# By-token rows: v loaded once a batch into a ring of pairs, turned tiles in six named places, and splits and pieces tied to the score tiles

## The chip, the cores and the metric

One core of one Trainium2 chip. The metric is device time in microseconds (us) of one execution, the median of several runs.

## The reference

For each of 8 batches of 2496 tokens, with u and v of 256 columns and z of 64:

```
scores = (1/S) * z @ z.T
out    = u * (max(scores, 0)**2 @ v)          # x, 19968 rows of 256
logits = normed(x) @ normed(expert_emb).T / tau     # 8 experts
y[t]   = p_top(t) * (max(x[t] @ w1[e], 0) @ w2[e])  # e = the token's best expert
```

The expert part is computed for the best expert of each token alone, so tokens have to be sorted by expert.

## The kernel before

**Two stages.** The first stage computes attention batch by batch, gates it with u and routes each token: its row goes by an indirect DMA into a table sorted by expert. The second stage runs the experts over slots of that table. The change is in the first stage.

**Numbers in pairs.** Each float32 operand is split into two float16 parts (high and low), after a scaling by a power of two. So z has tiles z1 and z2 (`z_split`), v has rows `vv` of high and low parts (`v_split`, ScalarE writes the high part, VectorE the low), and the squared scores have `hl` (`parts`). The scaling needs the largest absolute value of z and of v of the whole batch before the first split: `scan_load` brings a piece of z or v, `scan_max` reduces it, and `scale_pieces` makes the power of two, with two small matmuls in between.

**Steps.** A batch is 5 groups g of (up to) 512 tokens, and each group runs over 20 rows s of 128 keys: 100 steps a batch, 800 in all. The `for i, (b, g, q, s)` loop is the program order; PE follows it exactly. A step multiplies one tile of squared scores with a row of v (`values`, L361 to L370). Since scores are symmetric, only tiles with s // 4 >= g are computed (`scores`: L269 and L270 on PE, L272 and L273 on ScalarE; `parts`: L306 and L307 on VectorE, L302 and L303 for the short group). Those are 20, 16, 12, 8 and 4 of the 20 steps of the five groups; they are made three and two such steps ahead. For the tiles of later groups SP sends a transposing DMA (L319, L321) from `hl` into `tt`, which a later group reads. So the first group of a batch computes 20 tiles and turns 18 of them, the last computes four and turns none.

**Beside the steps.** For the next batch, a list `todo` made by `ahead` holds pieces with a step at which they are due: scans, scale pieces, z loads, z splits and z copies. v comes twice: 8 scan loads of 320 KB a batch (L107, reduced on L114), then 20 row loads of 128 KB (`v_load`, L201) into 6 buffers `vt`, each load four rows ahead of its split (L238, L239). `queue` holds the pieces of the routing of the last group (L411 to L525), among them four transposing DMAs of the gated rows (L449, `rowt`). `wq` holds the preparation of the expert weights (L562 to L625).

**Who sets the order.** PE is in program order. On the other engines and on SP, which issues nearly all DMAs, a scheduler orders the instructions by when it believes them ready; `tc.issue_after(x)` makes instructions stand behind x on their engine. Before, `todo` pieces stand behind the latest score tile on ScalarE and VectorE (`state["at"]`, `state["dv"]`), and `u` and weight DMAs behind the latest transposing DMA (`behind_moves`). Row loads, splits of v and `queue` pieces are free. Each engine and each DMA queue then takes its instructions strictly in that order.

Of the kernel before, what the change touches and what calls it, by code (L numbers as in the profile page):

```python
# [7 lines left out]
F32 = mybir.dt.float32  # L8
# [11 lines left out]
P = 128  # L20
# [3 lines left out]
VAHEAD = 4  # L24
# [20 lines left out]
def relu2_attention_then_moe(ctx, tc, zT, u, v, emb, tau, w1, w2, ident, tri, iota_e, out):  # L45
# [46 lines left out]
    zraw = {}  # L92


    ZSCANS, VSCANS = 2, 2 * D // DQ
    SCAN = SP * DQ // (P * ZSCANS)
    assert SP * DQ == ZSCANS * SCAN * P and DQ % ZSCANS == 0 and SP % VSCANS == 0
    scan = {}

    def scan_load(b, what, i, eng=None):  # L100

        t = wk.tile([P, SCAN], F32, name="scan", tag="scan", bufs=2)
        if what == "z":
            src = zT[b, i * (DQ // ZSCANS):(i + 1) * (DQ // ZSCANS), :]
        else:
            src = v[b, i * (SP // VSCANS):(i + 1) * (SP // VSCANS), :]
        (eng or nc.sync).dma_start(t, src.rearrange("a c -> (a c)").rearrange("(p w) -> p w", p=P))  # L107
        scan[b, what, i] = t

    def scan_max(b, what, i):  # L110
        if i == 0:
            n = ZSCANS if what == "z" else VSCANS if b else NV0
            scan[b, what] = sml.tile([P, n], F32, name="smx" + what)
# [3 lines left out]
    SCANS = [("z", i) for i in range(ZSCANS)] + [("v", i) for i in range(VSCANS)]  # L117
# [44 lines left out]

    def z_tiles(b):
# [12 lines left out]
    def z_split(b, c0):  # L176
# [7 lines left out]
        nc.scalar.activation(z1[lo, c], zt[lo, :w], AF.Copy, scale=k[lo])  # L184
        if b == 0:
            nc.scalar.activation(z2[hi, c], zt[hi, :w], AF.Copy, scale=k[hi])
        nc.vector.scalar_tensor_tensor(z2[lo, c], zt[lo, :w], k[lo], z1[lo, c], op0=ALU.mult, op1=ALU.subtract)
# [9 lines left out]
    vraw = {}  # L197
# [6 lines left out]
    VC = 4  # L204
    NV0 = ceil_div(NST, VC)
    v0 = []

    def v_first(i):

        if not v0:  # L210
            assert NST * D <= 3 * min(W1, W2)
            v0.extend([wp.tile([P, W1], F32, name="v0a", tag="wr1"), wp.tile([P, W2], F32, name="v0b", tag="wr2"),
                       wp.tile([P, 2 * max(W1, W2)], F16, name="v0c", tag="wo").bitcast(F32)])
        per = min(W1, W2) // D
        assert per % VC == 0
        q = i * VC
        n = min(VC, NST - q)
        t = v0[q // per][:, q % per * D:(q % per + n) * D].rearrange("p (j d) -> p j d", d=D)
        nc.sync.dma_start(t, v[0, q * P:(q + n) * P, :].rearrange("(j p) d -> p j d", p=P))
        for j in range(n):  # L220
            vraw[0, q + j] = t[:, j, :]
        scan[0, "v", i] = t.rearrange("p j d -> p (j d)")

    def v_split(b, s):
        vt = vraw.pop((b, s))
        vv = vring.tile([P, 2 * D], F16, name="vv", tag="vv")
# [10 lines left out]
        else:  # L237
            nc.scalar.activation(vv[:, 0:D], vt, AF.Copy, scale=k)  # L238
            nc.vector.scalar_tensor_tensor(vv[:, D:], vt, k, vv[:, 0:D], op0=ALU.mult, op1=ALU.subtract)  # L239
        Vs[b, s] = vv  # L240

    state = {"pm": False, "sp": None}

    def behind_moves():
        return tc.issue_after(state["sp"]) if state["sp"] else ExitStack()
# [3 lines left out]
    turned = {}  # L249
    joint = {}  # L250
# [13 lines left out]
    def scores(b, g, s):  # L264
# [7 lines left out]
        state["at"] = nc.scalar.activation(a[:, :n], sc[:, :n], AF.Relu, scale=2.0 ** -SHIFT).ins  # L272
# [12 lines left out]
    def parts(b, g, s, a):  # L285
# [12 lines left out]
        else:  # L298
# [3 lines left out]
            state["dv"] = nc.vector.tensor_copy(hl[:, :n], a[:, :n]).ins  # L302
# [3 lines left out]
        state["dv"] = nc.vector.tensor_copy(oh, src).ins  # L306
# [926 lines left out]
```

## Time and profile before

| | us |
|---|---|
| median of 3 runs | 2185.7 |
| lowest and highest run | 2184.86, 2188.75 |
| the profiled execution, its own time | 2187.64 |
| its span in the profile | 2185.9 |
| first stage, to the first expert matmul | 1340.4 |
| second stage | 845.5 |

The span leaves out 1.7 us of the execution's own time. PE's busy share is 96%, but matmuls are pipelined and their ends are modelled, so how full PE is has to be read from how long equal amounts of matmuls take. The stretches below are cut at the first `acc` matmul of a batch or of a group.

### The profile page before, as it was taken

The page shows a single profiled execution, that of the slowest core. Times are in us where ns is not written, and L with a number is a line of the kernel's source. Part 1 is how long each engine was busy: PE and PEld are TensorE (multiplying, and loading weights), DVE is VectorE, ACT ScalarE, POOL GpSimd, SP SyncE. Part 2 cuts the span into 40 slices and gives each one's busy share as a digit, 9 for nine tenths or more (in the row PEclk, how much of TensorE's full clock was granted, in tenths as well). Part 3 has the DMA queues.
Part 4 walks back from the last instruction along what each step waited for, and adds up shares of the span by engine and source line. Part 5 has one row for each costly group of instructions (what it writes and reads, how often), then busy time and mean ns, then how long its engine had stood idle before and what let it go on. Part 6 is the DMA issues. An engine that isn't in the chain of part 4 may idle for free.

```text
span 2185.9 us, 50968 instructions
## 1 busy us (share of the span) xinstructions
PE 2103.3 (96%) x19210; PEld 1779.6 (81%) x19210; DVE 1334.7 (61%) x3976; ACT 1017.4 (47%) x2131; POOL 332.0 (15%) x344
## 2 busy tenths in 40 slices
PE   6999999999999999999999999999999999999998
PEld 4787787787777777787777788888888888888898
DVE  8777887887877877876877865533333333333333
ACT  7566566566566566666656653222222222222221
POOL 0011011101101111011011011212111121111111
PEclk9999999999999999999999999999999999999999
DMA  7977988989978978988977877433333333247584
GB/s 179 204 167 184 213 175 191 215 170 189 215 152 186 198 173 176 196 186 173 191 168 159 161 151 180 128 86 89 81 65 88 88 91 57 50 110 201 130 215 116
DMA packets 668860, 335.99 MB, mean 154 GB/s; under 512 B 564662, under 2 KB 637375, under 8 KB 662465
## 3 DMA queue, kind: packets, MB, share of 16 engines
q1 hardware_dynamic: 653136, 291.06, 61.8%
q0 software_dynamic: 15184, 41.24, 6.8%
q8 instruction: 152, 2.49, 0.5%
q14 instruction: 100, 0.81, 0.1%
q10 hardware_dynamic: 288, 0.39, 0.1%
HBM read 273.46 MB, written 59.60 MB: 152 GB/s over the span
## 4 chain that ended last, share of the span: by engine, by line
PE 69%; DVE 13%; DMA 10%; issue 3%; ACT 3%; SPq 2%; another core or an unknown queue 0%; DVEq 0%; POOL 0%; POOLq 0%; ACTq 0%
PE acc L361 8%; PE acc L365 8%; PE acc L363 8%; PE po L974 6%; PE po L972 6%; PE po L973 6%; DMA scan<-in_v_dram 4%; PE sc L270 2%; PE sc L269 2%; DVE smxv L114 1%; DMA zt<-in_zT_dram 1%; SPq L449 1%; DVE vv L239 1%; DVE x L411 1%; DMA vt<-in_v_dram 1%
## 5 line engine op out<-in xcount | busy, mean ns | idle before, releaser
L272 ACT ACTIVATE a<-sc 128x512 f32<-128x512 f32 (+1 forms) x480 | 267.7, 558 | 242.9 <-PE sc L270 155.7
L525 POOL DMA_INDIRECT xs<-row,dsti x160 | 171.0, 1069 | 1075.6 <-ACT row L445 318.2
L273 ACT ACTIVATE a<-a 128x512 f32<-128x512 f32 (+1 forms) x480 | 286.3, 596 | 12.6
L361 PE MATMUL acc<-vv,tt 128*128 128x256 f16 x1152 | 269.2, 273 | 0.5 <-DVE lg L462 0.4
L363 PE MATMUL acc<-vv,tt 128*128 128x256 f16 x1152 | 269.1, 272 | 0.5 <-issue 0.5
L979 POOL DMA_INDIRECT out_dram<-ot,me x159 | 155.1, 975 | 659.2 <-DVE ot L978 626.0
L972 PE MATMUL po<-w,hh 128*128 128x256 f16 x928 | 253.0, 273 | 0.0
L974 PE MATMUL po<-w,hl 128*128 128x256 f16 x928 | 253.0, 273 | 0.0
L973 PE MATMUL po<-w,hh 128*128 128x256 f16 x928 | 253.0, 273 | 0.0
L978 DVE TENSOR_SCALAR ot<-po,me,w 128x256 f32<-128x256 f32 x116 | 58.3, 540 | 215.5 <-PE po L974 205.5
L269 PE MATMUL sc<-z 128*128 128x512 f16 (+1 forms) x480 | 175.6, 366 | 9.5 <-ACT a L272 6.3
L365 PE MATMUL acc<-vv,tt 128*128 128x256 f16 x1152 | 178.2, 273 | 0.4 <-issue 0.4
L270 PE MATMUL sc<-z,z 128*128 128x512 f16 (+1 forms) x480 | 175.7, 366 | 0.0
L974 PEld LDWEIGHTS <-hl 128*128 128x128 f16 x1272 | 124.5, 98 | 14.5
L973 PEld LDWEIGHTS <-hh 128*128 128x128 f16 x1272 | 124.5, 98 | 14.2
L972 PEld LDWEIGHTS <-hh 128*128 128x128 f16 x1272 | 124.5, 98 | 14.2
L361 PEld LDWEIGHTS <-tt 128*128 128x128 f16 x1152 | 112.5, 98 | 14.3 <-DVE lg L462 0.9
L363 PEld LDWEIGHTS <-tt 128*128 128x128 f16 x1152 | 112.6, 98 | 13.9 <-issue 1.1
L365 PEld LDWEIGHTS <-tt 128*128 128x128 f16 x1152 | 112.6, 98 | 13.5 <-issue 0.5
L239 DVE SCALAR_TENSOR_TENSOR vv<-vt,scv,vv 128x256 f16<-128x256 f32 x133 | 61.4, 477 | 53.1 <-ACT vv L238 52.8
L974 PE MATMUL po<-wb,hl 128*128 128x256 f16 x344 | 93.8, 273 | 0.0
L972 PE MATMUL po<-wb,hh 128*128 128x256 f16 x344 | 93.8, 273 | 0.0
(5249 smaller groups left out, 5498.4 us busy)
## 6 DMA issues: line engine op xcount, KB each, us to landing
w<-wsd SPq DMA_DIRECT2D x64, 1026.0 KB
wa<-wsd SPq DMA_DIRECT2D x46, 1024.0 KB
w<-wsd SPq DMA_DIRECT2D x42, 1024.0 KB
wb<-wsd SPq DMA_DIRECT2D x24, 1026.0 KB
ut<-in_u_dram SPq DMA_DIRECT2D x72, 256.0 KB
vt<-in_v_dram SPq DMA_DIRECT2D x140, 128.0 KB
scan<-in_v_dram SPq DMA_DIRECT2D x56, 320.0 KB
wr<-in_w_dram SPq DMA_DIRECT2D x64, 256.0 KB
```

Of the source, the lines that this page charges most:

```text
L269: nc.tensor.matmul(sc[:, :n], z1[:, ss], z1[:, t0:t0 + n], start=True, stop=False)
L270: nc.tensor.matmul(sc[:, :n], z1[:, ss], z2[:, t0:t0 + n], start=False, stop=True)
L272: state["at"] = nc.scalar.activation(a[:, :n], sc[:, :n], AF.Relu, scale=2.0 ** -SHIFT).ins
L273: nc.scalar.activation(a[:, :n], a[:, :n], AF.Square)
L361: nc.tensor.matmul(outs[j], piece(ph, j), vh, start=first and j % 2 == 0, stop=False, skip_group_check=True)
L363: nc.tensor.matmul(outs[j], piece(ph, j), vl, start=False, stop=False, skip_group_check=True)
L365: nc.tensor.matmul(outs[j], piece(pl, j), vl if last else vh, start=False, stop=ends, skip_group_check=True)
L525: put = nc.gpsimd.indirect_dma_start(xs[:, :], bass.IndirectOffsetOnAxis(ap=loc["dsti"][:m, j:j + 1], axis=0), row[:m, j, :], None)
L972: nc.tensor.matmul(o, hh[:, f, t], wh, start=(f == 0), stop=False)
L973: nc.tensor.matmul(o, hh[:, f, t], wl, start=False, stop=False)
L974: nc.tensor.matmul(o, hl[:, f, t], wh, start=False, stop=(f == NF - 1))
L979: put = nc.gpsimd.indirect_dma_start(out, bass.IndirectOffsetOnAxis(ap=me.bitcast(U32)[:, j, 1:2], axis=0), ot[:, j, :], None, bounds_chec ...
```

## The change

`v` is loaded once a batch: `scan_load` for v brings two rows of 128 keys (256 KB) into a tile of the same ring `vring` that holds the split rows, `scan_max` reduces that tile, and `v_split` later reads it from there. The ring has 22 places for a raw or a split pair. Row loads and their 6 buffers are gone; the scan buffer is one of half the size, and z is scanned in four pieces instead of two.

```
-    vring = actx.enter_context(tc.tile_pool(name="vring", bufs=NST + 5))
+    NVP = NST // 2
+    vring = actx.enter_context(tc.tile_pool(name="vring", bufs=2 * NVP + 2))
-    tp = actx.enter_context(tc.tile_pool(name="tp", bufs=min(7, max(1, NG * (NG - 1) // 2))))
+    tp = actx.enter_context(tc.tile_pool(name="tp", bufs=1))
+    places = [f"tt{i}" for i in range(6)]
...
-    ZSCANS, VSCANS = 2, 2 * D // DQ
+    ZSCANS = 4
...
     def scan_load(b, what, i, eng=None):
-        t = wk.tile([P, SCAN], F32, name="scan", tag="scan", bufs=2)
...
+        if what == "v":
+            t = vring.tile([P, 2, D], F32, name="vr", tag="vv")
+            (eng or nc.sync).dma_start(t, v[b, 2 * i * P:2 * (i + 1) * P, :].rearrange("(j p) d -> p j d", p=P))
+            for j in range(2):
+                vraw[b, 2 * i + j] = t[:, j, :]
+            scan[b, what, i] = t.rearrange("p j d -> p (j d)")
+            return
+        t = wk.tile([P, SCAN], F32, name="scan", tag="scan", bufs=1)
...
-    def v_load(b, s):
-        vt = wk.tile([P, D], F32, name="vt", tag="vt", bufs=VAHEAD + 2)
-        nc.sync.dma_start(vt, v[b, s * P:(s + 1) * P, :])
-        vraw[b, s] = vt
```

A score tile's ScalarE work now stands behind the last split on ScalarE, and its VectorE work behind the last split on VectorE (`state["as"]` and `state["ds"]` are set in `z_split` and `v_split`, from the second batch's splits on). `todo` DMAs stand behind the latest transposing DMA, and `queue` and weight pieces behind the latest score tile:

```
+            if b:
+                state["as"], state["ds"] = hi_, lo_
...
+        with behind("as"):
+            state["at"] = nc.scalar.activation(a[:, :n], sc[:, :n], AF.Relu, scale=2.0 ** -SHIFT).ins
...
+        with behind("ds"):
+            state["dv"] = nc.vector.tensor_copy(oh, src).ins
...
-                with tc.issue_after(state["at"]), tc.issue_after(state["dv"]):
+                with tc.issue_after(state["at"]), tc.issue_after(state["dv"]), behind_moves():
                     todo.pop(0)[2]()
         values(accs[b, g], b, g, q, s, *half(b, g, s))
         if queue:
-            queue.pop(0)()
+            with tc.issue_after(state["at"]), tc.issue_after(state["dv"]):
+                queue.pop(0)()
...
-                with tc.issue_after(state["dv"]), behind_moves():
+                with tc.issue_after(state["at"]), tc.issue_after(state["dv"]), behind_moves():
                     wq.pop(0)()
```

The scans are due earlier and are spread wider, the splits of the next batch's v are due two steps ahead instead of four, and a turned tile takes the place that has been free longest of six, instead of a rotation of seven:

```
-    early = 4
+    early = 2
...
-        at = min(NST + 4, NB // 4)
-        for i, what in enumerate(SCANS):
-            todo.append((at + 2 * i, False, lambda w=what: scan_load(b + 1, *w)))
-            todo.append((at + 2 * i + 4, False, lambda w=what: scan_max(b + 1, *w)))
-        at += 2 * len(SCANS) + 4
+        for i in range(ZSCANS):
+            todo.append((6 * i, False, lambda i=i: scan_load(b + 1, "z", i)))
+            todo.append((6 * i + 5, False, lambda i=i: scan_max(b + 1, "z", i)))
+        for i in range(NVP):
+            todo.append((3 * i + 2, False, lambda i=i: scan_load(b + 1, "v", i)))
+            todo.append((3 * i + 14, False, lambda i=i: scan_max(b + 1, "v", i)))
+        at = 3 * NVP + 14
...
+                place_[b, g, h] = places.pop(0)
+                turned[b, g, h] = tp.tile([P, 2 * GT, 512], F16, name="tt", tag=place_[b, g, h])
...
+        if c == GT - 1:
+            places.append(place_.pop((b, h, g)))
```

At the start, the first batch's v comes in ten loads of 256 KB, five from SP and five from ScalarE's queue, instead of five of 512 KB from SP, and is reduced in ten pieces.

How the order moves is shown at three places.

ScalarE, at the end of the fifth batch (number 4), from the last rows of the last group to the first score tile behind them. `vv` and `vh` are the splits of the next batch's v, `row_100` a routing piece, `a<-sc` the score tile of the last own step. Before:

```order
L238 ACTIVATE vv<-vt,scv 128x256
L445 ACTIVATE row_100<-x,up 128x256
L238 ACTIVATE vv<-vt,scv 128x256 x5
L234 ACTIVATE vh<-vt,scv 64x256
L238 ACTIVATE vv<-vt,scv 128x256 x3
L232 ACTIVATE vv<-vt,scv 64x256
L272 ACTIVATE a<-sc 128x448
```

Now:

```order
L418 ACTIVATE sq,n_12937<-x 128x256 x3
L192 ACTIVATE z_10782<-zt,scz 64x256
L441 ACTIVATE row_100<-x,up 128x256 x3
L192 ACTIVATE z_10782<-zt,scz 64x256
L441 ACTIVATE row_100<-x,up 128x256
L263 ACTIVATE a<-sc 128x448
```

The splits of v no longer stand ahead of that tile. They are now in the fourth group of the batch, ahead of its first own score tile, again on ScalarE:

```order
L223 ACTIVATE vv<-vr,scv 128x256 x3
L441 ACTIVATE row_99<-x,up 128x256 x4
L219 ACTIVATE vh<-vr,scv 64x256
L618 ACTIVATE wo<-wr_10676,wup 128x512
L223 ACTIVATE vv<-vr,scv 128x256 x9
L217 ACTIVATE vv<-vr,scv 64x256
L263 ACTIVATE a<-sc 128x512
```

Before, four weight pieces stood at that place and five splits of v further ahead.

SP, in the first group of the next batch (number 5). `tt` are turned score tiles, `rowt` turned gated rows. Before:

```order
L319 DMA_TRANSPOSE tt<-hl__13692 128x8x128
L562 DMA wr_13360<-in_w_dram 128x512
L449 DMA_TRANSPOSE rowt<-row_99 128x4x128
L319 DMA_TRANSPOSE tt<-hl__13725 128x8x128
L449 DMA_TRANSPOSE rowt<-row_99 128x4x128 x3
L319 DMA_TRANSPOSE tt<-hl__13754 128x8x128
L319 DMA_TRANSPOSE tt<-hl__13802 128x8x128
L379 DMA ut<-in_u_dram 128x2x256
```

Now:

```order
L313 DMA_TRANSPOSE tt<-hl__13689 128x8x128
L445 DMA_TRANSPOSE rowt<-row_99 128x4x128
L313 DMA_TRANSPOSE tt<-hl__13715 128x8x128
L445 DMA_TRANSPOSE rowt<-row_99 128x4x128
L313 DMA_TRANSPOSE tt<-hl__13740 128x8x128
L445 DMA_TRANSPOSE rowt<-row_99 128x4x128
L107 DMA vr<-in_v_dram 128x2x256
L313 DMA_TRANSPOSE tt<-hl__13768 128x8x128
L445 DMA_TRANSPOSE rowt<-row_99 128x4x128
L114 DMA scan<-in_zT_dram 128x320
```

The turned rows come about five tiles later and one by one, and between the first and the last of the group's 16 `tt` transposes there are now six loads of v and two of z, with one more z load ahead of them, where none were.

## Rows read from the trace of the kernel before

**Rows 1.** The head of the profile's page: busy us of PE, its share of the span, and the row loads of v.

```profile
PE 2103.3 (96%) x19210; PEld 1779.6 (81%) x19210; DVE 1334.7 (61%) x3976; ACT 1017.4 (47%) x2131; POOL 332.0 (15%) x344
...
vt<-in_v_dram SPq DMA_DIRECT2D x140, 128.0 KB
```

**Rows 2.** The view of windows, one window for each batch (0 to 7): window, its length, then busy us and instructions of each engine, the granted clock as a share of 2.4 GHz, the DMA share and GB/s.

```profile
23.50:188.40 164.90, 159.92 (x1371) 128.36 (x1371) 130.10 (x424) 109.21 (x238) 13.42 (x14) 0.98 0.80 174
188.40:349.10 160.70, 157.02 (x1397) 128.10 (x1398) 128.16 (x423) 101.97 (x224) 22.85 (x22) 1.00 0.88 193
349.10:510.90 161.80, 156.76 (x1398) 128.36 (x1398) 127.55 (x426) 103.30 (x227) 22.57 (x22) 1.00 0.91 191
510.90:678.70 167.80, 158.21 (x1397) 127.74 (x1396) 126.81 (x424) 101.97 (x226) 21.45 (x22) 1.00 0.87 185
678.70:847.30 168.60, 158.19 (x1396) 127.57 (x1396) 127.13 (x421) 101.57 (x224) 21.70 (x22) 1.00 0.86 184
847.30:1013.00 165.70, 157.71 (x1397) 128.27 (x1396) 127.89 (x426) 103.17 (x227) 22.09 (x22) 1.00 0.91 186
1013.00:1183.20 170.20, 159.81 (x1396) 128.74 (x1396) 127.34 (x425) 101.48 (x226) 21.41 (x21) 0.99 0.83 173
1183.20:1340.40 157.20, 153.95 (x1382) 126.97 (x1383) 110.29 (x390) 89.91 (x192) 20.85 (x20) 1.00 0.82 162
```

**Rows 3.** The same view, the last group of batches 0 to 6.

```profile
159.50:188.40 28.90, 26.88 (x250) 22.33 (x248) 19.33 (x70) 19.03 (x46) 5.09 (x6) 1.00 0.72 189
322.30:349.10 26.80, 26.40 (x250) 22.48 (x248) 19.41 (x71) 16.57 (x40) 5.19 (x5) 1.00 0.80 208
484.60:510.90 26.30, 26.30 (x250) 22.47 (x248) 19.04 (x68) 16.70 (x42) 4.36 (x5) 1.00 0.86 207
649.90:678.70 28.80, 27.09 (x249) 22.40 (x247) 20.16 (x75) 15.52 (x41) 4.25 (x5) 1.00 0.77 196
818.80:847.30 28.50, 26.84 (x249) 22.26 (x246) 18.16 (x64) 13.91 (x36) 4.57 (x5) 1.00 0.69 188
982.70:1013.00 30.30, 27.25 (x250) 22.41 (x247) 18.06 (x67) 14.54 (x38) 4.73 (x5) 1.00 0.75 180
1152.80:1183.20 30.40, 27.26 (x249) 22.47 (x246) 18.95 (x68) 14.35 (x38) 4.54 (x5) 1.00 0.68 146
```

**Rows 4.** ScalarE and SP's queue in order of time around 840 us, the end of batch 4: start, length, line, what it writes and reads, and in brackets the idle time before it and what ended it.

```profile
839.20 5.67 SPq L201 DMA_DIRECT2D vt<-in_v_dram  x7
...
841.53 0.50 ACT L234 ACTIVATE vh<-vt,scv 64x256 f16<-64x256 f32 x1 [7.06 <-DMA vt<-in_v_dram]
842.06 1.31 ACT L238 ACTIVATE vv<-vt,scv 128x256 f16<-128x256 f32 x3
...
843.67 0.52 ACT L272 ACTIVATE a<-sc 128x448 f32<-128x448 f32 x1
```

**Rows 5.** The view of windows again, the third group of batches 1, 3, 4, 5 and 6.

```profile
260.50:292.60 32.10, 32.09 (x288) 26.46 (x288) 28.81 (x100) 19.92 (x44) 3.93 (x4) 1.00 0.95 216
...
582.80:617.50 34.70, 32.86 (x291) 26.63 (x290) 29.43 (x107) 22.23 (x48) 4.29 (x5) 1.00 0.85 177
752.00:789.60 37.60, 32.94 (x291) 26.70 (x291) 29.66 (x110) 21.69 (x47) 4.18 (x5) 1.00 0.81 168
918.30:953.00 34.70, 32.65 (x291) 26.50 (x288) 28.77 (x102) 20.45 (x43) 4.08 (x5) 1.00 0.92 200
1086.00:1123.60 37.60, 33.98 (x289) 27.04 (x286) 30.00 (x102) 21.59 (x47) 3.90 (x4) 0.95 0.79 177
```

**Rows 6.** The view of waits, 100 to 1340 us, over all engines: who waited for whom, us in total, times, the longest.

```profile
DVE smxv L114 <- DMA scan<-in_v_dram: 31.4, 27, 2.9
...
ACT wo L622 <- DMA wsd<-wo: 6.9, 3, 3.2
...
PE pm L128 <- DVE smv L126: 3.7, 3, 2.9
```

**Rows 7.** SP's queue in order of time in the first group of batch 5 (847.3 to 885.0 us).

```profile
852.31 1.23 SPq L319 DMA_TRANSPOSE tt<-hl__13611  x1
853.64 1.29 SPq L319 DMA_TRANSPOSE tt<-hl__13634  x1
854.98 0.58 SPq L379 DMA_DIRECT2D ut<-in_u_dram  x1
...
861.79 4.32 SPq L449 DMA_TRANSPOSE rowt<-row  x3
866.20 1.26 SPq L319 DMA_TRANSPOSE tt<-hl__13754  x1
...
883.12 2.16 SPq L319 DMA_TRANSPOSE tt<-hl__14030  x1
```

**Rows 8.** The view of waits in that group.

```profile
DVE hl__13914 L306 <- DMA tt<-hl__13754: 4.2, 1, 4.2
...
PE acc L361 <- DVE hl__13914 L306: 1.8, 1, 1.8
```

**Rows 9.** ScalarE in order of time in the fourth group of batch 4, the first own score tile behind the routing pieces.

```profile
806.08 0.60 ACT L272 ACTIVATE a<-sc 128x512 f32<-128x512 f32 x1 [5.13 <-PE sc L270]
```

**Rows 10.** The groups of instructions by line, VectorE: the reduces of 512 and 1024 elements (busy us, mean ns of one).

```profile
L573 DVE TENSOR_REDUCE mx<-wr 128x1 f32<-128x512 f32 x64 | 43.1, 678 | 1.0 <-DMA wr<-in_w_dram 0.7
...
L114 DVE TENSOR_REDUCE smxv<-v0a 128x1 f32<-128x1024 f32 x2 | 2.3, 1214 | 0.0
```

More of the change, by code (lines that the diff above doesn't have):

```diff
@@ L195, in z_copy @@
         nc.sync.dma_start(z2[DQ:P, c], z1[0:DQ, c])
-    vraw = {}
-    def v_load(b, s):
-        vt = wk.tile([P, D], F32, name="vt", tag="vt", bufs=VAHEAD + 2)
-        nc.sync.dma_start(vt, v[b, s * P:(s + 1) * P, :])
-        vraw[b, s] = vt
[L204 to L222, printed above, removed]
     def v_split(b, s):
         vt = vraw.pop((b, s))
-        vv = vring.tile([P, 2 * D], F16, name="vv", tag="vv")
+        if s % 2 == 0:
+            vpair[b] = vring.tile([P, 2, 2 * D], F16, name="vv", tag="vv")
+        vv = vpair[b][:, s % 2, :]
         k = scan[b, "cv"]
@@ L305, in parts @@
             return hi, lo
-        state["dv"] = nc.vector.tensor_copy(oh, src).ins
+        with behind("ds"):
+            state["dv"] = nc.vector.tensor_copy(oh, src).ins
         nc.vector.tensor_tensor(ol, src, oh, op=ALU.subtract)
@@ L309, in parts @@
             if (b, g, h) not in turned:
-                turned[b, g, h] = tp.tile([P, 2 * GT, 512], F16, name="tt", tag="tt")
+                place_[b, g, h] = places.pop(0)
+                turned[b, g, h] = tp.tile([P, 2 * GT, 512], F16, name="tt", tag=place_[b, g, h])
             m = min(P, S - s * P)
@@ L645, in relu2_attention_then_moe @@
     first.__enter__()
-    for what, i in SCANS[:ZSCANS]:
-        scan_load(0, what, i, nc.scalar if i % 2 else nc.sync)
+    z0 = wp.tile([P, W1], F32, name="z0", tag="wr1")
+    for i in range(2):
+        t = z0[:, 2 * i * SCAN:2 * (i + 1) * SCAN]
+        src = zT[0, i * (DQ // 2):(i + 1) * (DQ // 2), :]
+        (nc.scalar if i % 2 else nc.sync).dma_start(t, src.rearrange("a c -> (a c)").rearrange("(p w) -> p w", p=P))
+        scan[0, "z", i] = t
     nc.scalar.dma_start(idt, ident)
@@ L652, in relu2_attention_then_moe @@
         z_load(0, k * ZC)
-    for i in range(NV0):
-        v_first(i)
+    for i in range(NVP):
+        scan_load(0, "v", i, nc.scalar if i % 2 else nc.sync)
     z_load(0, 2 * ZC)
-    for what, i in SCANS[:ZSCANS]:
-        scan_max(0, what, i)
+    for i in range(2):
+        scan_max(0, "z", i)
     for f in scale_pieces(0, "z"):
@@ L666, in relu2_attention_then_moe @@
         probs[direct[i]] = scores(*direct[i])
-    for i in range(NV0):
+    for i in range(NVP):
         scan_max(0, "v", i)
-        if i == NV0 - 2:
+        if i == NVP - 3:
             halves[direct[0]] = parts(*direct[0], probs.pop(direct[0]))
@@ L701, in relu2_attention_then_moe @@
     trib = cst.tile([P, P], BF16, name="trib")
-    tri_f = wk.tile([P, D], F32, name="tri_f", tag="vt", bufs=VAHEAD + 2)[:, 0:P]
+    cpair = [vring.tile([P, 2, D], F32, name=f"cpair{i}", tag="vv") for i in range(2)]
+    tri_f = cpair[0][:, 0, 0:P]
     nc.sync.dma_start(tri_f, tri)
@@ L708, in relu2_attention_then_moe @@
     nc.sync.dma_start(iot, iota_e)
-    emb_sb = wk.tile([P, D], F32, name="emb_sb", tag="vt", bufs=VAHEAD + 2)[:E]
+    emb_sb = cpair[0][:E, 1, :]
     nc.sync.dma_start(emb_sb, emb)
@@ L713, in relu2_attention_then_moe @@
     itau = cst.tile([P, 1], F32, name="itau")
-    esq = wk.tile([P, D], F32, name="esq", tag="vt", bufs=VAHEAD + 2)[:E]
+    esq = cpair[1][:E, 0, :]
     en2 = sml.tile([E, 1], F32, name="en2", bufs=1)
     ede = sml.tile([E, 1], F32, name="ede", bufs=1)
-    en = wk.tile([P, D], F32, name="en", tag="vt", bufs=VAHEAD + 2)[:E]
+    en = cpair[1][:E, 1, :]
     carry = sml.tile([P, E], F32, name="carry", bufs=3)
@@ L1096, in relu2_attention_then_moe @@
             ecap0 = ecap[0:1, :]
-            behind.close()
+            held.close()
         if b == 0 and g == 0:
```

53 lines of the change are left out of this document (25 added, 28 removed).

## The prediction

> **What bounds the kernel now.** The page comes first: PE is busy for 96% of the span and no other engine for more than 61% [rows 1]. A reader should see two things in that. PE sets the end, so a change that leaves PE's matmuls alone can only give back time in which PE stands still. And busy time will not say how much that is, because overlapping ends of matmuls count as busy. So the second view is windows over equal amounts of work [rows 2]. Batches 1 to 6 hold the same matmuls, within one or two, yet take 160.7 to 170.2 us. Batch 7, which prepares no next batch, takes 157.2. The spread of 9.5 us is therefore waiting, and it belongs to what is done beside the matmuls: the change works on just that. The second stage, 845 us, is untouched.
>
> Where in a batch the waiting lies is read from windows on groups. The last group of a batch takes 26.3 us in batch 2 and up to 30.4 in batch 6, with the same 250 matmuls [rows 3]. The reason stands in the order of time at the end of batch 4 [rows 4]: ScalarE sits idle for 7.06 us because a row of v has not landed, SP still being at seven row loads, and the score tile on L272 that PE needs next stands behind those splits. The third group takes 32.1 us in batch 1 and 34.7 to 37.6 in batches 3 to 6 [rows 5]; there the waits name several things at once [rows 6]: VectorE waits for scan loads (31.4 us in all, 27 times), ScalarE for the weights' store buffer (6.9 us, three times), and PE for the small reductions before a transpose (3.7 us, three times, the longest 2.9, in batch 6).
>
> **The change, part by part.** All figures are against the profiled execution, 2187.64 us for a span of 2185.9. The median of the runs is 1.9 us lower than that execution.
>
> *Row loads of v go.* 140 loads of 128 KB [rows 1] and the wait for them disappear; in their place 70 loads of 256 KB, which also serve the scan, come a group or more ahead of the splits. In the new order of ScalarE no split stands ahead of the last score tile of a batch, so the 7 us wait of [rows 4] has nothing left to wait for. Next in line there are four routing rows and z splits, which stood there before too. Over the shortest last group, 26.3 us, batches 0 to 6 lose 2.6 + 0.5 + 0 + 2.5 + 2.2 + 4.0 + 4.1 = 15.9 us [rows 3]. I leave 0.4 us a batch in place and take **-13 us**; bounds -6 (another late piece keeps the rest) and -16.
>
> *Scans and pieces in the middle.* Loads now come 12 steps ahead of a v reduction, where they came four, so VectorE's 31.4 us of waiting for scan data should go, and pieces tied behind the latest score tile cannot be put ahead of it. But the small reductions, their matmuls and the weights' store buffer stay as they are. Over batch 1's 32.1 us the third groups of batches 3 to 6 lose 2.6 + 5.5 + 2.6 + 5.5 = 16.2 us [rows 5]. I cannot split that between what goes and what stays, so I take half, **-8 us**; bounds 0 and -16.
>
> *The first group gets loads that it did not have.* Here the change costs. SP issues one transposing DMA each 1.33 us and one plain load each 0.6 us or so, and from 852.3 us to 885.3 us of a group that lasts 37.7 us its queue is without a pause; the three `rowt` transposes take 4.32 us together, and the `tt` transpose behind them starts at 866.2 [rows 7]. What is late then is shown too: VectorE waits 4.2 us for that DMA to give back an `hl` buffer, and PE loses 1.8 us [rows 8]. The change puts nine loads more (six of v, three of z) into that stretch: 9 x 0.58 = 5.2 us, so 33.0 + 5.2 = 38.2 us of issue in 37.7 us. On the other side the `rowt` transposes come one by one and about five tiles later, so no block of three holds up a `tt` any more. Bounds: 0, if spreading pays for the loads, and 7 x 5.2 = +36 us, if every microsecond of issue reaches PE. I take the overrun of the totals, 0.5 us in each of seven batches, **+3.5 us**, since the queue has 4.7 us of pause a group to absorb the rest. The later `rowt` is read by the logits at the 18th step; issued one by one up to the 13th or 14th, it has four steps of 37.7 / 20 = 1.9 us to land, and I book nothing. The Trainium skill, DMA: Bandwidth & Descriptors, section Issuing engines are not separate DMA queues, says that the time to initiate a DMA is usually small relative to the DMA itself. By that, issue would not bind, and this term would be 0; the trace's 1.3 us for each of a row of transposes without a pause speaks against it here.
>
> *Splits of v move into the fourth group.* In the new order ten splits more stand ahead of that group's first own score tile, ten times 1.31 / 3 = 0.44 us [rows 4], 4.4 us in all. ScalarE was idle for 5.13 us just there [rows 9], so they are hidden, with 0.7 us to spare; PE's need for that tile is three steps later still. If the cover is gone, the tile is late by what exceeds it: I book 0, upper bound +1 us a batch.
>
> *The start.* Ten reductions of 512 elements (0.678 us) replace five of 1024 (1.214 us) [rows 10]: 6.8 against 6.1, on the path to the first `acc` matmul, **+0.7 us** (0 to +2, since ScalarE's queue now issues five of the loads ahead of the first split of z).
>
> *With one answer, nothing:* the scans cost VectorE 0.6 us more a batch (by the line through [rows 10], ten of 512 and four of 320 elements take 8.7 us, ten of 640 took 8.1), under some 33 us of its idle time in a batch [rows 2]; six places for turned tiles are enough, since never more than six are unread at once; ties of score tiles to splits cost only if a split waits, and its data is then long there.
>
> Sum: -13 - 8 + 3.5 + 0.7 = -16.8, so 2187.6 - 16.8 = 2170.8, and at the median's distance **2169 us**.
>
> **The rivals.**
>
> *SP's queue becomes the bound in the first group (slower).* Place: seven first groups. Mechanism: the `tt` transposes fall behind by the issue time of the added loads, `hl` buffers come back late, VectorE and then PE wait, as in [rows 8]. Price at most +36 us: 2187.6 - 21 + 36 + 0.7 - 1.9 = 2202 us. It decides from (13 + 8 - 0.7) / 7 = 2.9 us a batch, more than half of the added issue. For it: the queue without a pause [rows 7]. Against: it had that already, and PE lost only some 2 us.
>
> *Issue time does not bind there.* Transposes wait for their data, not for the queue, and the first-group term is 0: 2169 - 3.5 = 2165 us. For it: SP's queue still has 4.7 us of pause in the group. It is what the page's sentence would make of it.
>
> *The waits only change their names (no change).* Third groups keep all their waits, the last groups keep half, since the routing rows and z splits that stay ahead of the last tile are late in place of v: -6.5 + 3.5 + 0.7 = -2.3, 2183 us. For it: the wait list of the third group has three causes and the change removes one.
>
> *Every batch runs like batch 1.* The scheduler's order suits the chip in batch 1 and less in later ones; if ties keep it, all batches take 160.7 us: 1.1 + 7.1 + 7.9 + 5.0 + 9.5 = 30.6 us less in batches 2 to 6 [rows 2], some 2155 us, and a few us less if the last groups reach 26.3 everywhere.
>
> **How the numbers follow.** Forecast 0.47, issue time not binding 0.15, like batch 1 0.12, no change 0.14, SP's queue 0.12. A measurement of this kernel can tell about 0.2%, 4.4 us. The first three are faster by more, and I add 0.04 of the fourth: 0.78. Same 0.10, slower 0.12. The range 2148 to 2187 takes in the rival near 2155 with its few us and the case of no change, up to the third groups giving nothing and the start costing its bound, and leaves out the slower rival.
>
> **What would show it.** Right: last groups near 26.6 us in every batch, no ScalarE wait for v; no VectorE wait for a v scan; batches of nearly equal length; first groups within 1 us of 37.7, and 38 us at most. Wrong: first groups of 40 us or more with VectorE's wait for `tt` DMAs grown; third groups still at 35 to 37 us with PE waiting for the small matmuls' reductions; a ScalarE wait ahead of the fourth group's first own tile gone and PE idle there.

## The result and the profile after

The change makes the kernel slower, by 0.7%. Its median is 2200.2 us (2192.95 to 2206.7, 6 runs) beside 2185.3 us of the kernel before in the same comparison (2182.9 to 2188.75, 6 runs): ratio 1.0068, 95% interval 1.0045 to 1.009. The forecast was 2169 us, faster. In the profiled executions the span goes from 2185.9 to 2196.1 us and the mean granted clock from 0.996 to 0.987 of 2.4 GHz.

The span's 10.2 us are divided here by the start of the first `acc` matmul of each group, summed over the batches; batch 0's first group stands apart, since the start shows there:

| us | to the first `acc` | batch 0, first group | first groups 1 to 7 | second | third | fourth | last | second stage |
|---|---|---|---|---|---|---|---|---|
| before | 23.5 | 37.4 | 265.1 | 276.2 | 274.7 | 238.9 | 224.6 | 845.5 |
| the change | 25.8 | 42.7 | 287.6 | 291.1 | 258.9 | 236.0 | 208.0 | 846.0 |
| difference | +2.3 | +5.3 | +22.5 | +14.9 | -15.8 | -2.9 | -16.6 | +0.5 |

So the change does give what it was priced for, and more: 35.3 us less in the third, fourth and last groups. It then gives 37.4 us back in the first and second groups and 7.6 us at the start.

The view of windows of the changed kernel: the last groups of batches 0, 3, 4 and 6, the third groups of batches 1, 3, 4 and 6, and the first groups of batches 0, 1, 5 and 7 (window, its length, then busy us and instructions of PE, PEld, DVE, ACT and POOL, granted clock, DMA share, GB/s).

```profile
165.85:192.06 26.21, 26.21 (x249) 22.63 (x247) 16.32 (x65) 12.43 (x31) 6.48 (x4) 1.00 0.59 137
...
667.71:693.92 26.21, 26.21 (x250) 22.64 (x248) 16.00 (x64) 11.83 (x30) 5.71 (x4) 1.00 0.63 136
836.17:862.38 26.21, 26.21 (x249) 22.64 (x247) 15.88 (x64) 11.54 (x29) 3.84 (x4) 1.00 0.57 140
...
1166.46:1192.67 26.21, 26.21 (x250) 22.64 (x247) 15.94 (x65) 10.32 (x27) 3.85 (x4) 1.00 0.56 137
...
270.30:302.39 32.09, 32.09 (x290) 26.56 (x288) 25.09 (x93) 19.27 (x45) 3.84 (x4) 1.00 0.78 156
...
605.93:638.55 32.62, 32.62 (x293) 26.84 (x290) 25.67 (x104) 19.32 (x44) 3.94 (x5) 1.00 0.66 130
773.14:806.29 33.15, 32.78 (x293) 26.77 (x291) 25.77 (x103) 19.62 (x46) 3.94 (x5) 1.00 0.67 131
...
1104.74:1137.05 32.31, 32.26 (x289) 26.46 (x287) 22.77 (x82) 17.75 (x41) 3.84 (x4) 1.00 0.82 165
...
25.81:68.50 42.69, 37.65 (x276) 28.12 (x276) 38.88 (x108) 34.21 (x69) 0.31 (x1) 0.92 0.77 153
192.06:233.87 41.81, 36.20 (x298) 28.39 (x297) 31.48 (x91) 28.25 (x59) 4.25 (x4) 0.96 1.00 208
...
862.38:905.03 42.65, 37.64 (x298) 28.72 (x297) 32.24 (x95) 26.40 (x55) 3.84 (x4) 0.92 1.00 197
...
1192.67:1229.93 37.26, 34.74 (x299) 27.79 (x297) 30.13 (x90) 26.40 (x55) 4.14 (x4) 1.00 0.95 171
```

The last groups answer to [rows 3]: all are 26.21 us and PE is busy in all of it. The third groups answer to [rows 5]: 34.7 and 37.6 us have become 32.1 to 33.2. The first groups are the loss: 41.8 and 42.7 us, with PE idle for some 5 us, and a granted clock under 1.

What PE waits for is plain in the groups of instructions by line (count, busy us, mean ns; behind the bar the idle time just before and what ended most of it), first of the kernel before, 100 to 1340 us, then of the changed one, 100 to 1350 us; and in the changed kernel's view of waits, 100 to 1340 us (us in total, times, longest):

```profile
L457 PE MATMUL pt<-e,rowt 128*128 128x16 f16 x608 | 21.4, 170 | 1.4 <-DMA rowt<-row 1.4
```

```profile
L453 PE MATMUL pt<-e,rowt 128*128 128x16 f16 x608 | 24.2, 170 | 46.3 <-DMA rowt<-row 46.3
```

```profile
PE pt L453 <- DMA rowt<-row: 46.3, 21, 3.8
...
DVE smxz L121 <- DMA scan<-in_zT_dram: 35.8, 14, 5.6
```

The logits matmuls (`pt`) wait 46.3 us for the turned rows, where it was 1.4 us before. 29.6 us of it stand in first groups and the rest in second groups. Another wait has shrunk: in the view of PE's waits, 20 to 1350 us, the lines of `acc` behind VectorE's `hl` add up to 30.8 us (52 waits) before and to 3.5 us (5 waits) now. VectorE's wait for v's scans [rows 6] is gone, but the z scans, now in one buffer, wait 35.8 us in its place: 27.5 us in first groups and 8.3 us in second groups. No wait of PE there is put down to them.

One such stall, in order of time in the first group of batch 5 (862.4 to 905.0 us), the stretch of [rows 7]. ScalarE's last two splits of the gated rows, then SP's queue, then PE's logits (start, length, line, what is written and read, in brackets the idle time before and what ended it):

```profile
881.14 0.50 ACT L441 ACTIVATE row<-x,up 128x256 f16<-128x256 f32 x1
882.88 0.50 ACT L441 ACTIVATE row<-x,up 128x256 f16<-128x256 f32 x1
```

```profile
883.43 0.53 SPq L107 DMA_DIRECT2D vr<-in_v_dram  x1
884.06 1.39 SPq L313 DMA_TRANSPOSE tt<-hl__13689  x1
885.56 1.21 SPq L445 DMA_TRANSPOSE rowt<-row  x1
...
890.89 1.23 SPq L445 DMA_TRANSPOSE rowt<-row  x1
892.17 0.58 SPq L107 DMA_DIRECT2D vr<-in_v_dram  x1
892.84 1.23 SPq L313 DMA_TRANSPOSE tt<-hl__13768  x1
894.17 1.24 SPq L445 DMA_TRANSPOSE rowt<-row  x1
```

```profile
892.08 0.35 PE L453 MATMUL pt<-e,rowt 128*128 128x16 f16 x8
893.52 0.26 PE L453 MATMUL pt<-e,rowt 128*128 128x16 f16 x4 [1.09 <-DMA rowt<-row]
897.62 0.27 PE L453 MATMUL pt<-e,rowt 128*128 128x16 f16 x4 [3.83 <-DMA rowt<-row]
```

Two delays add up. The splits, tied behind score tiles, run one a step and end at 883.4 us, 21 us into the group. SP then sends the `rowt` 7 to 11 us after their splits end, because tiles and loads stand between them in a queue without a pause. The last leaves SP at 895.4; PE, in program order, has been standing since 893.8.

The second delay is not new. In the kernel before, the last split and the logits of the same group, with the last `rowt` of [rows 7] between them (SP was done with it at 866.1):

```profile
859.43 0.50 ACT L445 ACTIVATE row<-x,up 128x256 f16<-128x256 f32 x1
...
879.88 0.55 PE L457 MATMUL pt<-e,rowt 128*128 128x16 f16 x16
```

Over the first groups of batches 1 to 7, SP took up the last `rowt` 5 to 12 us after the last split had ended, and now 8 to 11 us after it. But before, that split ended 12 to 13 us into the group, and the last `rowt` left SP 7 to 14 us ahead of the last logits. Now it ends some 8.5 us later, and the spare time is used up. The tie does this: the split ends 21 to 22 us into the group in e4, a kernel of the next section that has the tie alone, and 10 to 12 us in e1, which has all but the tie.

Behind the stall the clock is down. The view of windows, 2 us each:

```profile
894.00:896.00 2.00, 0.00 (x0) 0.00 (x0) 0.33 (x2) 0.00 (x0) 0.00 (x0) 1.00 1.16 266
896.00:898.00 2.00, 0.38 (x5) 0.24 (x6) 0.00 (x0) 0.00 (x0) 0.00 (x0) 0.52 1.05 164
898.00:900.00 2.00, 2.00 (x9) 1.21 (x8) 1.93 (x5) 1.17 (x2) 0.00 (x0) 0.50 1.21 296
900.00:902.00 2.00, 2.00 (x10) 1.09 (x8) 1.76 (x10) 0.67 (x3) 0.00 (x0) 0.50 0.90 214
902.00:904.00 2.00, 2.00 (x14) 1.45 (x13) 1.97 (x7) 0.69 (x2) 0.00 (x0) 0.78 1.34 42
```

In the stall the granted clock falls to 0.50, the lower of its two levels (1.2 GHz), and PE then makes 9 or 10 matmuls in 2 us where it makes 20 from 904 to 906 us, at full clock again. Two windows at 0.50 and one at 0.78 cost 2 x 1.0 + 0.44 = 2.4 us behind a stall of 3.8 us.

At the start there is a stall of another kind, in order of time on PE:

```profile
41.71 0.27 PE L357 MATMUL acc<-vv,hl__405 128*128 128x256 f16 x1 [3.39 <-ACT vv L223]
```

PE stands for the split of the first batch's 7th row of v, which before came in time. ScalarE, in order of time, made the first six splits by 27.8 us, and the 7th only behind the one instruction of the block of small constants:

```profile
40.25 0.40 ACT L1079 ACTIVATE cpair<-cpair 8x256 f32<-8x256 f32 x1
...
41.17 1.69 ACT L223 ACTIVATE vv<-vr,scv 128x256 f16<-128x256 f32 x4
```

This stall too is followed by matmuls at half clock: from 44 to 46 us the granted clock is 0.50 and PE makes 10.

### The profile page after: what moved, and what is told of

Same layout as the page of the kernel before. It is cut to its first block, busy times and chain, and to the rows that moved or that the text cites. A ratio compares the mean times of both kernels' runs of the same rounds, so it can differ in the third digit from the quotient of the medians.

```text
span 2196.1 us, 50747 instructions
## 1 busy us (share of the span) xinstructions
PE 2106.9 (96%) x19210; PEld 1794.6 (82%) x19210; DVE 1333.8 (61%) x4009; ACT 1014.2 (46%) x2131; POOL 334.0 (15%) x344
## 4 chain that ended last, share of the span: by engine, by line
PE 83%; DMA 7%; DVE 6%; issue 1%; ACT 1%; SPq 1%; DVEq 0%; ACTq 0%; POOL 0%; POOLq 0%
PE acc L357 12%; PE acc L361 12%; PE acc L359 12%; PE po L974 6%; PE po L973 6%; PE po L975 6%; PE sc L259 4%; PE sc L260 3%; DMA rowt<-row 2%; PE acc L364 1%; PE acc L366 1%; PE pt L453 1%; DVE smxv L121 1%; DMA scan<-in_zT_dram 0%; DMA zt<-in_zT_dram 0%
## 5 line engine op out<-in xcount | busy, mean ns | idle before, releaser
L973 PE MATMUL po<-wb,hh 128*128 128x256 f16 x344 | 93.8, 273 | 0.0
L974 PE MATMUL po<-wb,hh 128*128 128x256 f16 x344 | 93.8, 273 | 0.0
```

What stands on the lines that cost most here:

```text
L973: nc.tensor.matmul(o, hh[:, f, t], wh, start=(f == 0), stop=False)
L974: nc.tensor.matmul(o, hh[:, f, t], wl, start=False, stop=False)
```

## The experiments

Two theories to begin with. **One**: the tie of `queue` pieces behind the score tiles makes the turned rows late. **Two**: the added loads fill SP's queue in the first group, and the rows stand behind them. The first four kernels ran on one chip. Ratios are to the kernel before on the same chip, with 95% intervals; waits for `rowt` are rows of the same view as above, 100 us to the end of the first stage.

**e1_free_queue**: the tie removed.

```
-            with tc.issue_after(state["at"]), tc.issue_after(state["dv"]):
-                queue.pop(0)()
+            queue.pop(0)()
```

> The changed kernel with the routing pieces of the queue free again (not behind the latest score tile); loads and all other ties as changed. Theory 1 (the tie makes the turned gated rows late, PE waits for them at the logits): PE's wait for rowt falls from 50.9 us to under 5, the half-clock stretches behind it go too, first groups 37 to 38.5 us, time 2135 to 2155. Theory 2 (the added loads fill SP's queue in the first group and the turned rows stand behind them whatever their order): at least 25 us of the wait stay, time above 2170.

Measured: 2186.3 us, ratio 0.9996 (0.9985 to 1.0007). The wait is nearly gone, the time is that of the kernel before, not under it. The row of the logits, and the view of waits in the first group of batch 5:

```profile
L453 PE MATMUL pt<-e,rowt 128*128 128x16 f16 x608 | 21.3, 169 | 6.8 <-DMA rowt<-row 6.8
```

```profile
DVE hl__13740 L299 <- DMA tt<-hl__13576: 3.3, 1, 3.3
...
DVE hl__13768 L299 <- DMA tt<-hl__13626: 2.5, 1, 2.5
DVE hl__13794 L299 <- DMA tt<-hl__13661: 2.4, 1, 2.4
```

The 50.9 us in the expectation stand in no view here; over the whole span the changed kernel's wait is 48.2 us. In this group the rows go early again, and now the `tt` transposes are late, as in [rows 8] but three times in a row. In most first groups only the splits go early: they end 10 to 12 us into the group, but in five of the seven the last `rowt` leaves SP only 28 to 32 us into it, just ahead of the logits. SP's queue in the first group of batch 1, which starts at 190.0 us and has its logits at 220.2:

```profile
215.45 2.58 SPq L445 DMA_TRANSPOSE rowt<-row  x2
```

In e6, where no load of the next batch stands in these groups, SP takes up the last `rowt` 15 to 22 us into them, here 20 to 31. First groups of batches 1 to 7 take 273.2 us. So theory one is right on the wait, and theory two is right that the loads hold the rows up on SP, though PE had to wait for them only 6.8 us.

**e2_late_loads**: the tie kept, the loads moved out of the first group.

```
-            todo.append((6 * i, ...scan_load(b + 1, "z", i)
+            todo.append((20 + 6 * i, ...
-            todo.append((3 * i + 2, ...scan_load(b + 1, "v", i)
+            todo.append((21 + 2 * i, ...
-        at = 3 * NVP + 14
+        at = 50
```

> The changed kernel with the tie kept and the loads of z and v moved out of the first group (steps 20 to 39, reductions to step 47). Theory 1: the turned rows are still one per step up to the 14th step, over half of the wait stays (25 us or more), time above 2170. Theory 2: SP's queue is relieved of 5 us a batch ahead of the last turned row, the wait falls below 10 us, time 2140 to 2160.

Measured: 2195.9 us, ratio 1.0038 (1.0022 to 1.0054).

```profile
L453 PE MATMUL pt<-e,rowt 128*128 128x16 f16 x592 | 23.2, 170 | 34.1 <-DMA rowt<-row 34.0
```

The wait for `rowt` stays at three quarters without any load of the next batch in the first group. In first groups alone it falls from 29.6 to 15.7 us, while in second groups, where the loads now stand, it goes from 18.6 to 20.5 us (with that of batch 0, which stands ahead of 100 us). Theory two falls as the whole cause of that wait; by this it is half of it in the first groups.

**e3_loads_act**: the tie kept, the next batch's loads issued on ScalarE's queue.

```
-... scan_load(b + 1, "z", i)))
+... scan_load(b + 1, "z", i, nc.scalar)))
-... scan_load(b + 1, "v", i)))
+... scan_load(b + 1, "v", i, nc.scalar)))
```

> The changed kernel with the tie and the early loads kept, but the loads of the next batch's z and v issued by ScalarE's queue instead of SP's: the same bytes at about the same steps, no SP issue time. If SP's issue time is what makes the rows late (theory 2 as a matter of issue): wait below 10 us, time 2140 to 2160. If the transfers slow each other: no change, 2195 to 2205. Theory 1: over 25 us of the wait stay, above 2170.

Measured: 2186.8 us, ratio 1.0001 (0.9987 to 1.0015).

```profile
L453 PE MATMUL pt<-e,rowt 128*128 128x16 f16 x608 | 23.4, 170 | 29.5 <-DMA rowt<-row 29.4
```

Second groups fall from 291.1 to 270.7 us, first groups of batches 1 to 7 do not (291.8). In those of batches 1 to 6 the last split of the rows ends 24 to 26 us into the group, not 21: ScalarE itself now waits, 18.7 us in all for `rowt` transposes; e5 shows one such wait.

**e4_before_tied**: the kernel before, with the tie of `queue` alone (the edit of e1, reversed).

> The kernel before with the tie of the routing pieces alone. Theory 1: PE waits for rowt in first and second groups as in the changed kernel, 30 us or more, time 2210 to 2235. Theory 2: without the added loads the rows come in time, at most 8 us more than before, 2185 to 2194.

Measured: 2229.5 us, ratio 1.0178 (1.0151 to 1.0205).

```profile
L457 PE MATMUL pt<-e,rowt 128*128 128x16 f16 x608 | 25.3, 170 | 41.5 <-DMA rowt<-row 41.5
```

Theory one is shown from the other side. Those two lines alone, in a kernel with none of the change's loads in the first group, cost 1.8%, some 39 us, and bring the wait for `rowt` with them.

Theory two, in a new form, for the second four: the loads are a cost of their own, hidden as long as the rows are late. Those kernels ran on another chip, where the kernel before took 2193.3 us (2187.6 us beside the first four).

**e5_free_act**: the edits of e1 and e3 together.

> The change with two edits together: the routing pieces untied (as in e1_free_queue) and the next batch's z and v loads issued from ScalarE's queue (as in e3_loads_act). Theory (two costs that cover each other): the tie makes the turned rows late, and the added loads make SP's queue too full, so that hl buffers come back late; each edit alone left the other's wait. Then both waits go: PE behind rowt under 10 us and PE behind hl (L299, L300) under 12 us in all, first groups of batches 1 to 6 at 36 to 38.5 us, time 2155 to 2168 us. Rival (the first group is bound by the transfers, not by the issue on SP): first groups stay at 38.4 to 41 as in e1_free_queue, PE behind hl stays near 30 us, time 2180 to 2187.

Measured: 2173.9 us, ratio 0.9903 (0.9869 to 0.9938). By the ratio the gain, some 21 us, is at the low end of the expected one (2155 to 2168 beside the 2187.6 us of the first four is 20 to 33 us); the profiled execution (2183.7 us) was the longest of the four. PE's wait for `rowt` is gone, but its lines behind `hl` add up to 26.7 us where under 12 were expected, and first groups still take 36.6 to 42.8 us in batches 1 to 6. ScalarE and SP in order of time in the first group of batch 3 show one reason:

```profile
531.92 6.12 SPq L445 DMA_TRANSPOSE rowt<-row  x3
...
541.73 1.22 SPq L445 DMA_TRANSPOSE rowt<-row  x1
542.93 0.37 ACTq L107 DMA_DIRECT2D vr<-in_v_dram  x1
```

```profile
543.35 0.63 ACT L264 ACTIVATE a<-a 128x512 f32<-128x512 f32 x1 [7.43 <-DMA rowt<-row]
```

The load now stands among ScalarE's own work, and waits there for a `rowt` transpose of SP; with it ScalarE's score tiles wait 7.4 us. In the trace the load and that transpose use the same semaphore (the counter by which a transfer reports its end), and the load goes out 0.02 us after the transpose's last count: the program makes it wait. The load left SP's queue and blocked an engine instead.

**e6_free_late**: the edits of e1 and e2 together.

> The change with the routing pieces untied and the next batch's loads moved to steps 20 to 39, where they stood before (all on SP). Theory (SP's issue in the first group): the first group is as before the change, 37 to 39.5 us in batches 1 to 6, PE behind hl falls under 12 us of its 31 in e1_free_queue; second groups pay by 0 to 2 us each; time 2162 to 2178. Rival (the transfers bind, wherever the loads stand): first groups gain what second groups lose, time 2182 to 2190.

Measured: 2170.6 us, ratio 0.9904 (0.9872 to 0.9937). The view of windows, first groups of batches 1 and 3:

```profile
193.41:228.98 35.57, 34.94 (x298) 27.46 (x297) 29.02 (x85) 28.25 (x59) 5.00 (x4) 1.00 0.99 187
...
518.13:553.56 35.43, 34.99 (x298) 27.42 (x297) 27.96 (x82) 26.14 (x55) 4.69 (x4) 1.00 1.03 189
```

First groups of batches 1 to 6 are 35.3 to 36.1 us, shorter than before the change (37.2 to 39.7) and at full clock. With e1 and e2 this is a square: taking the tie away is worth 0.7% with the loads early and 1.3% with the loads late; moving the loads is worth 0.3% with the tie and 0.9% without. The ratios come from three comparisons and have intervals of 0.1 to 0.3% to either side, so the 0.3% is hardly clear of noise. Both edits together give 1.6%, the two alone 1.0% in sum; that is clear of the intervals, if narrowly. Each cost hides part of the other.

**e7_rows_earlier**: the tie kept, the pieces ahead of the splits packed closer.

```
-[none, gate_x, none, both(fold, one(square, 0)), one(square, 1), one(square, 2), one(square, 3), root, scale]
+[none, gate_x, both(fold, one(square, 0), one(square, 1)), both(one(square, 2), one(square, 3)), root, scale]
```

> The change with the tie kept, but the routing's pieces ahead of the logits packed closer (two squares in one step, one empty step dropped): the four splits and their rowt transposes are issued three steps earlier, 3 x 1.9 = 5.7 us, the logits stay at the 18th step. Theory (rows late by the tie, a lateness of 1 to 5 us at the logits): PE's wait for rowt falls from about 51 us to under 15 us, and the SP-bound wait for hl shows in its place (20 to 35 us), as in e1_free_queue; time 2180 to 2192. Rival (rowt is late because SP's queue is behind, not because of its place): the wait for rowt stays over 35 us, time 2195 to 2203.

Measured: 2207.1 us, ratio 1.0058 (1.0034 to 1.0083), above the range expected. The row of the logits:

```profile
L453 PE MATMUL pt<-e,rowt 128*128 128x16 f16 x608 | 21.1, 170 | 0.0
```

The wait for `rowt` is gone altogether, with the tie in place and the splits ending some 4 us earlier (16.6 to 17.4 us into the first groups). The time did not follow: first groups of batches 1 to 7 fall to 271.4 us, second groups rise to 306.0. As expected, another wait stands in its place: PE's lines behind `hl` add up to 39.4 us (3.5 in the change), half of it in the second groups. So one wait took the other's place. In the second groups PE stands still for 28.7 us in all where it was 19.9 in the change, which makes up 9 of the 15 us by which they grew; the rest was not traced.

**e8_consts_later**: e5 with a block of small constants moved from step 6 to 16, its second part from 14 to 20, against the stall of the 7th row at the start.

> e5_free_act with the small constants of routing (the block of some 25 VectorE instructions and one on ScalarE at step 6, and its second part at step 14) ten and six steps later, which puts two to four splits of v ahead of score tiles where ScalarE had none between about 28 and 41 us. Theory (batch 0's first group is long because its splits of v come in a bunch): that group falls from about 43 us to 38 to 40, PE's wait for vv at its 7th step goes, and the time is 3 to 5 us under e5_free_act. Rival (it is long for the z loads or for the loads of batch 1 in it): it stays at 42 to 44 us and the time is that of e5_free_act.

Measured: 2181.2 us, ratio 0.9948 (0.993 to 0.9965). Batch 0's first group is 48.0 us, not 38 to 40, and the time is 7 us above that of e5: the theory of the start seemed to fall. But ScalarE has its own loads between the splits here, so two things differ; the next kernels leave the loads on SP.

**e9_free_late_consts**: e6 with that block at steps 20 and 24. It ran with e10 and e11 beside a kernel before of 2189.3 us.

```
-        if i == 6:
+        if i == 20:
-        if i == 14:
+        if i == 24:
```

> e6_free_late with the block of small constants of routing moved from step 6 to step 20 and its second part from step 14 to step 24, which lets the first batch's splits of v stand one by one between the score tiles on ScalarE, where they stood in a bunch behind that block. Theory (batch 0's first group is long because PE waits for the split of its 7th row): that wait, 5 us in e6_free_late, goes with the half clock behind it, batch 0's first group falls from 44.8 us to 37 to 39, the rest stays, ratio to the kernel before 0.986 to 0.989. Rival (the group is long for another cause, the loads of the start or of z): it stays at 43 to 45 us and the ratio at 0.990.

Measured: 2162.6 us, ratio 0.9865 (0.9845 to 0.9884). The same stretch, 38 to 43 us, in e6 and then in e9:

```profile
38.00:43.00 5.00, 0.34 (x2) 0.06 (x1) 4.28 (x15) 4.52 (x11) 0.00 (x0) 0.98 0.77 159
43.00:48.00 5.00, 4.11 (x17) 2.41 (x17) 4.97 (x21) 3.61 (x10) 0.00 (x0) 0.50 0.74 157
```

```profile
38.00:43.00 5.00, 5.00 (x42) 3.90 (x40) 4.90 (x13) 4.95 (x12) 0.00 (x0) 1.00 0.85 159
```

Batch 0's first group falls from 44.8 to 36.7 us. In e6 PE makes 2 matmuls in the first window and 17 at half clock in the second; in e9 it makes 42.

**e10_spread**: e9 with the loads spread wider.

```
-            todo.append((20 + 6 * i, ...scan_load(b + 1, "z", i)
+            todo.append((18 + 5 * i, ...
-            todo.append((21 + 2 * i, ...scan_load(b + 1, "v", i)
+            todo.append((19 + 3 * i, ...
-        at = 50
+        at = 56
```

> e9_free_late_consts with the next batch's loads spread over steps 18 to 46 instead of 20 to 39, the scale pieces from step 56. Theory (issue on SP binds where transposes and loads stand together; second and third groups of batches 1 to 4 still lose 1 to 4 us each in e6_free_late): second groups fall by 0.5 to 1.5 us, third groups stay within 0.5 us, since they have a third fewer transposes than the second; ratio 0.984 to 0.987. Rival (what is left there are the small reductions and their matmuls, not the loads): second groups stay, and third groups grow by 0.5 to 1 us because the scale pieces end later; ratio 0.988 to 0.991.

Measured: 2153.7 us (2153.19 to 2158.15, 5 runs), ratio 0.9831 (0.9813 to 0.9849). This is the best kernel, 1.7% under the kernel before and, by the two ratios, some 2.4% under the change. First groups of batches 1, 3 and 5:

```profile
189.33:224.62 35.29, 34.78 (x298) 27.55 (x297) 29.07 (x86) 28.38 (x59) 5.00 (x4) 1.00 0.99 188
...
509.41:544.81 35.40, 35.10 (x299) 27.47 (x297) 28.03 (x83) 26.22 (x56) 4.69 (x4) 1.00 1.01 190
...
831.76:867.75 35.99, 34.76 (x299) 27.57 (x297) 28.63 (x86) 26.53 (x55) 5.36 (x4) 1.00 0.97 180
```

The reason given for it holds only in part: in the profiled executions second groups fell by 0.8 us in all, third groups by 4.8, and the second stage, where nothing differs, was 4.9 us shorter.

**e11_tied_consts**: the change with e9's edit alone.

> The change as it is, with only the block of small constants moved from steps 6 and 14 to steps 20 and 24. Theory (the wait for the 7th split is a cost of the start by itself): batch 0's first group falls from 42.7 us to 38 to 40, all other groups stay within 1 us, PE's wait for rowt stays over 40 us, and the time is 3 to 5 us under that of the change: ratio 1.004 to 1.006. Rival (the length of that group comes from the tie or from the loads): it stays over 42 us, ratio 1.006 to 1.008.

Measured: 2196.6 us, ratio 1.0027 (1.0016 to 1.0039), below the range expected. Batch 0's first group falls from 42.7 to 39.1 us; the wait for `rowt` stays at 42.4 us, first groups of batches 1 to 7 at 286.4.

**e12_spread_tied**: e10 with the tie put back.

> e10_spread with the tie of the routing pieces put back, and nothing else: no load of the next batch stands in the first group before its 18th step. Theory (the tie by itself makes the turned rows late, loads or no loads): PE's wait for rowt is 30 to 45 us where e10_spread has none, first groups of batches 1 to 6 are 37 to 40 us where they were 34.9 to 37.4, ratio to the kernel before 0.993 to 1.002. Rival (the tie only hurts where the loads already fill SP's queue): the wait is under 12 us and the ratio 0.983 to 0.988.

Measured: 2186.9 us, ratio 0.9985 (0.997 to 1.0), beside a kernel before of 2189.6 us on another chip.

```profile
L453 PE MATMUL pt<-e,rowt 128*128 128x16 f16 x592 | 23.2, 170 | 36.5 <-DMA rowt<-row 36.5
```

The tie alone takes back 1.5% of the best kernel, 34 us, with no load of the next batch in the first group's first 18 steps.

## Why the prediction was wrong

**The step that failed** is the last of the first-group term: "The later `rowt` is read by the logits at the 18th step; issued one by one up to the 13th or 14th, it has four steps of 37.7 / 20 = 1.9 us to land, and I book nothing." In batch 5 the splits run up to 21 us into the group, as the order had it. But SP is not at that point: it is 7 to 11 us behind, and the last transpose leaves it 33 us into the group, when PE already stands at the logits. The order of the instructions was read as a time. The working had itself shown SP's queue without a pause [rows 7], and counted its length for the `tt` tiles and not for the rows that were to join it; the kernel before already sent the last `rowt` 5 to 12 us after its split. A wait of 46.3 us, with the stretches at half clock behind it, stands against 35.3 us of gain elsewhere. e4 and e12 price the tie by itself: 39 and 34 us; with the early loads beside it, taking it away gives back 0.7%, some 16 us (e1).

**The second groups** have no term in the sum at all. The tie holds there too: the last split ends 19 to 21 us into them where it ended 6.5 to 8 before, some 17 us of the 46.3 stand there, and they are 14.9 us longer.

**First group, loads** (+3.5 us, bound +36): the size was off, and the cost was partly hidden behind the tie. Without the tie, the early loads cost 0.9% (e1 against e6), some 20 us, between the forecast and the bound. The totals of issue in the group, 38.2 us in 37.7, said that there was just room; room at the end of a group does not help a queue that is late in its middle. The wait that the term was priced by went the other way: PE's waits behind `hl` were 17.4 us in the first groups before, not the 1.8 us of one group [rows 8], and are 1.9 us with the change. Whether the rows coming one by one did that, or PE's standing at the logits, in which SP catches up, is not separated; e7, where the rows also come one by one and PE does not stand there, has 19.6 us.

**Issue time does not bind**, the rival worth 2165 us, falls with it. Taking fourteen loads a batch off SP, or later than the first group, made the kernel faster in e3, and in e5 and e6 against e1.

**Slower, by SP's queue** (2202 us): near in time by luck, since it adds -21 and +36 where -35.3, +37.4 and +7.6 were measured, and half right in mechanism. SP's queue was the bound, but what was late was `rowt` ahead of the logits and not `tt` ahead of `hl`; PE's waits behind `hl` stayed under those of the kernel before while the tie stood (3.5 us for 30.8), and came back only once it was taken away (e1: 21.1 us).

**Last groups** (-13 us): -16.6. Right, and the 0.4 us a batch that was left in place went too. **Third groups** (-8, bounds 0 and -16): -15.8. The bound was the answer: earlier scans and tied pieces together took all that could be taken. Which of the two did is not separated in full: without the tie (e1) half of it stays, 8.0 us, and the tie alone on the kernel before (e4) brings none (277.6 us). The reading behind the term was off: of the 31.4 us of waits for v's scans [rows 6], 23.5 us stood in second groups and only 8.0 us in third groups. **Fourth groups** (0): -2.9, no loss from the splits of v. **VectorE's scans**: the wait for v is gone as forecast; 35.8 us for z took its place unforeseen, in first and second groups.

**The start** (+0.7, up to +2): +2.3 to the first matmul, and +5.3 in batch 0's first group, which the term did not look at. There the order of ScalarE had changed too: the splits of v from the 7th row on stood behind the one instruction of the block of constants. e9 and e11 show it: moving that block gives back 8.0 and 3.6 us of that group.

What stays open: some 6 of the 15 us by which e7's second groups grow, and how much of e10's gain over e9 is its spread loads.

## What to carry to other kernels

When a change ties work behind other work, follow each thing that it makes late to its reader through every queue between them, and add the queue's own lateness: a place in the order is not a time on a queue that never pauses. Two causes of waiting on one path hide each other, so test the removal of both before giving up either; here each edit alone brought the time back to that of the kernel before at best, and both together 1.0% under it, or 1.7% with two smaller repairs. What costs a queue can be moved to where that queue has pauses; moved to an engine that computes, it can block the engine.

## What was not expected of the hardware

A stall of PE of 3.8 us was followed by about 6 us in which the granted clock was 0.50 and then 0.78, and this cost 2.4 us more. The executions in which PE waited 36 to 46 us for `rowt` had mean granted clocks of 0.983 to 0.990 (the change, e4, e11, e12), and e10, where it did not wait for it, 0.997.

A load issued from ScalarE stood 7.4 us until a transpose issued from SP had landed, and ScalarE's arithmetic stood with it (e5). Both use one semaphore, so this is the program's wait; that the hardware asks for it is not shown. The Trainium skill, DMA: Bandwidth & Descriptors, section Issuing engines are not separate DMA queues, says that DMAs of different engines share the same DMA engines and that issuing from several saves only the sequencer's time. No run here tests the first. The saving was not small here: with the loads off SP, second groups fell by 20 us (e3).
